# Linear attention as 24 groups of two pairs of heads, its matmuls on four 64x64 quarters, ahead of a gated MLP

## The chip, the cores and the metric

The kernel runs on one core of one Trainium2 chip. The core has a matrix engine (PE, with its weight loads shown as PEld), three engines for elementwise work (DVE, ACT, POOL), a queue for transfers (SP), a working memory of 128 partitions, and eight banks of 512 float32 columns per partition in which matmul results land (PSUM). The metric is device microseconds of one execution, the median of several runs.

## The reference, cut to what matters

There are 4 batches, 8 heads, 768 tokens and 48 channels per head. Attention keeps a 48x48 state for each batch and head; each token reads the state and its own contribution, weighted by the bonus `u`, and then decays the state by `w`:

```
for t in range(S):
    kt, vt, rt = (k[:, :, t], v[:, :, t], r[:, :, t])
    cur = np.einsum('bhd,bhe->bhde', u[None] * kt, vt)
    y[:, :, t] = np.einsum('bhd,bhde->bhe', rt, state + cur)
    state = w[None, :, :, None] * state + np.einsum('bhd,bhe->bhde', kt, vt)
```

Its output, 3072 tokens of 384 channels, goes through a gated MLP (called MoE in the code) with 1536 hidden channels:

```
gate = 1.0 / (1.0 + np.exp(-(x @ w_gate)))
val = x @ w_val
return (gate * val @ w_out).astype(np.float32)
```

## The kernel before, in words

**Attention.** The tokens are cut into 12 chunks of 64. A *burst* is one chunk of one pair of heads, all four batches: 48 bursts, four per chunk, in the order of the list `bursts`. With keys multiplied by inverse powers of the decay and queries by powers (table `tabk`), the attention inside a chunk becomes one masked score matrix of 64x64 for each batch and head, and everything earlier sits in the state. For burst n:

- `decayed` (L206) multiplies the keys by the table on DVE (L209), writes the decayed queries into the tile T on POOL (L212, a few on DVE) and multiplies query by key for the bonus on POOL (L215). `decayed_by_token` (L219) decays the keys in their token layout on POOL (L222).
- `bonus` (L224) multiplies by `u` and sums over channels on DVE (L228, L229). `diag` (L231) writes the sums as a diagonal matrix into the other half of T, in eight ACT instructions (L234).
- `scores` (L239) forms k times q for eight batch-and-head pairs: one head uses array rows 0 to 47 and output partitions 64 to 127, the other rows 64 to 111 and output partitions 0 to 63 (L245, L246). `outer` (L249) forms k times v for the state in the same two opposite corners (L255, L256).
- `post` (L258) copies the scores where the mask allows, over the diagonal, into T on DVE (L262), and decays and adds to the state, which lies in the tile vz beside the values, on DVE (L271, L273).
- `apply` (L278) multiplies state and values, stacked in the rows, by decayed queries and scores, stacked in the same way: eight matmuls over up to 128 rows, with two column halves (L283, L284). `to_x` (L286) splits the result into a rounded part (ACT, L300) and a rest (DVE, L301). For the fourth pair of heads these go to a separate tile xs, from which transfers on SP fill gaps in x (`fill`, L305).

**MLP.** Six tiles of 512 tokens (two chunks each) times 12 slices f of 128 hidden channels. An *item* is one slice of one tile. `up` (L323) is 18 matmuls in the float32r type (weights split into a high and a low part, three products for each of three row blocks, for gate and value). `gate` (L338) is a sigmoid on ACT (L343), a product on DVE (L344), a rounded copy on ACT (L345) and a rest on POOL (L346). `down` (L348) is nine matmuls into three accumulator banks (L356). The first tile runs its first four slices in halves of 256 tokens, eight half-width items and eight full ones. `store` (L365) copies the accumulators out in two halves (L368 on ACT, L369 on DVE) and sends them (L370).

**Weights** arrive as float64 words, are scaled on ACT (L175), joined to float32 in three DVE instructions (L181 to L183), rounded on ACT (L190) and subtracted on POOL (L191), in two halves for each of 12 slices. All of this falls into the first part of the run. `LOADW` and `DECW` say at which step each slice is loaded and decoded.

**Order.** The order on PE and SP is written out by hand; the other engines' order is chosen by the scheduler. `plan` lists the steps: five bursts alone (`PRE`), then items, with a burst in each of the first 11 and later in those which `SPREAD` marks (eight of twelve). In a step, `up` comes first (from the tenth step on), then the burst's scores and outer products, `apply` of the burst before, and `down` of the item before. Matmul results other than the accumulators share a ring of five single banks: `up` takes two, scores two, `apply` one.

Loads of a burst are one transfer of r and k in both layouts (L74), and for each chunk two transfers of v (L77, L78).

Of the kernel before, what the change touches and what calls it, by code (L numbers as in the profile page):

```python
# [10 lines left out]
F32 = mybir.dt.float32  # L11
# [9 lines left out]
P = 128  # L21
C = 64
# [8 lines left out]
PRE, HALF = NP + 1, 4  # L31
SPREAD = [1, 1, 1, 0, 1, 1, 1, 0, 1, 1, 0, 0]
EARLY = 9
LOADW = (-1, 1, 3, 4, 7, 9, 10, 11, 12, 13, 14, 15)
DECW = (1, 4, 5, 6, 9, 10, 11, 12, 13, 14, 15, 16)

U_POOL, R_DVE = range(3), range(4)
TILES = [[c, c + 1] for c in range(0, NC, 2)]
# [3 lines left out]
def rwkv_then_moe(ctx: ExitStack, tc: tile.TileContext, wd, un, rk, vn, wt, out):  # L42
# [6 lines left out]
    op = ctx.enter_context(tc.tile_pool(name="op", bufs=3))  # L49
    ps = ctx.enter_context(tc.tile_pool(name="ps", bufs=5, space=PSUM))  # L50
# [3 lines left out]
    att = main.enter_context(tc.tile_pool(name="att", bufs=4))  # L54
    att3 = main.enter_context(tc.tile_pool(name="att3", bufs=4))
    xp = main.enter_context(tc.tile_pool(name="xp", bufs=2))
    xsp = main.enter_context(tc.tile_pool(name="xsp", bufs=1))
# [6 lines left out]
    wu = const.tile([P, 2, NP], F32, name="wu")  # L64
    nc.sync.dma_start(out=wu, in_=wd)
    w = wu[:, 0]


    inp = {}
    vz = [const.tile([P, NP, 2, B, 64], F32, name=f"vz{i}") for i in range(2)]  # L70

    def load(c, p):
        inp[c, p] = att.tile([P, 2 * CT + 2 * B * D], F32, name="inp")
        nc.sync.dma_start(out=inp[c, p], in_=rk[c, p])  # L74

    def load_v(c):
        nc.sync.dma_start(out=vz[c % 2][64:128, :, 0], in_=vn[c, 64:128])  # L77
        nc.sync.dma_start(out=vz[c % 2][0:64, :, 1], in_=vn[c, 0:64])  # L78

    uns = const.tile([P, NP, D], F32, name="uns")  # L80
    ORDER = [NP - 1] + list(range(NP - 1))
    bursts = [(c, p) for c in range(NC) for p in ORDER]
    load(*bursts[0])
    load_v(0)
    nc.sync.dma_start(out=uns, in_=un)
    load(*bursts[1])
# [9 lines left out]
    cmask = causal.bitcast(I32)  # L96

    nc.vector.memset(vz[1][64:128, :, 1], 0.0)
    for t in (vz[0][0:64, :, 0], vz[0][64:128, :, 1], vz[1][0:64, :, 0]):
        nc.gpsimd.memset(t, 0.0)  # L100
    table = const.tile([P, 1], F32, name="table")
# [4 lines left out]
    pw = const.tile([P, NP, 97], F32, name="pw")  # L106
# [3 lines left out]
    def power(lo, n, by):  # L110
        nc.vector.tensor_tensor(
            pw[:, :, lo + 1 : lo + 1 + n], pw[:, :, 1 : 1 + n],
            pw[:, :, by : by + 1].broadcast_to([P, NP, n]), ALU.mult,
        )
# [7 lines left out]
    tabk = const.tile([P, NP, C], F32, name="tabk")  # L122
    nc.vector.tensor_copy(tabk[:, :, 0:32], pw[:, :, 31::-1])

    def inverses(p):
        nc.vector.reciprocal(tabk[:, p, 32:64], pw[:, p, 1:33])

    tabn = const.tile([P, NP, D], F32, name="tabn")
    flag = const.tile([1, 1], I32, name="flag")

    def token_table():

        power(32, 32, 32)
        power(64, 32, 64)
        tnat_in = hp.tile([P, 512], F32, name="sg").rearrange("q (p a j) -> q p a j", p=NP, a=2)
        for p in range(NP):
            nc.vector.tensor_copy(
                tnat_in[:, p], pw[:, p, 95:31:-1].unsqueeze(1).broadcast_to([P, 2, C])
            )
        tps = ps.tile([P, NP, P], F32, name="ring")  # L140
        for p in range(NP):
            nc.tensor.transpose(
                out=tps[:, p], in_=tnat_in[:, p].rearrange("q a j -> q (a j)"), identity=ident
            )
        nc.scalar.copy(out=tabn[0:64], in_=tps[0:64, :, 64:112])
        nc.scalar.copy(out=tabn[64:128], in_=tps[64:128, :, 0:48])

    def range_flag():
        good = const.tile([P, NP], F32, name="good")
# [4 lines left out]
        count = ps.tile([P, 512], F32, name="ring")  # L154
        nc.tensor.matmul(count[0:1, 0:NP], ones, good, start=True, stop=True)
        nc.vector.tensor_reduce(total, count[0:1, 0:NP], axis=mybir.AxisListType.X, op=ALU.add)
        nc.vector.tensor_scalar(flag, total, float(P * NP), None, ALU.is_lt)
# [34 lines left out]


    xt, xs, T, q, sc, yp = {}, {}, {}, {}, {}, {}

    def bc_b(ap):
        n, k = ap.shape
        return ap.unsqueeze(1).broadcast_to([n, B, k])

    def parts(n):  # L200
        c, p = bursts[n]
        t = inp[c, p][:, 0 : 2 * CT].rearrange("q (a b i) -> q a b i", a=2, b=B)
        u = inp[c, p][:, 2 * CT :].rearrange("q (a b d) -> q a b d", a=2, b=B)
        return c, p, t, u, vz[c % 2][:, p]

    def decayed(n):  # L206
        c, p, t, u, z = parts(n)
        T[n] = att3.tile([P, 2, B, C], F32, name="T")
        nc.vector.tensor_tensor(t[:, 1], t[:, 1], bc_b(tabk[:, p]), ALU.mult)  # L209
        for lo, k in ((0, 0), (64, 1)):  # L210
            eng = nc.vector if k and n in R_DVE else nc.gpsimd
            eng.tensor_tensor(  # L212
                T[n][lo : lo + 64, k], t[lo : lo + 64, 0], bc_b(tabk[lo : lo + 64, p, ::-1]), ALU.mult
            )
        nc.gpsimd.tensor_tensor(u[:, 0], u[:, 0], u[:, 1], ALU.mult)  # L215
        if n in U_POOL:
            nc.gpsimd.tensor_tensor(u[:, 0], u[:, 0], bc_b(uns[:, p]), ALU.mult)

    def decayed_by_token(n):  # L219
        c, p, t, u, z = parts(n)  # L220
        if c < NC - 1:
            nc.gpsimd.tensor_tensor(u[:, 1], u[:, 1], bc_b(tabn[:, p]), ALU.mult)  # L222

    def bonus(n):  # L224
        c, p, t, u, z = parts(n)
        q[n] = att.tile([P, B], F32, name="q")
        if n not in U_POOL:
            nc.vector.tensor_tensor(u[:, 0], u[:, 0], bc_b(uns[:, p]), ALU.mult)  # L228
        nc.vector.tensor_reduce(q[n], u[:, 0], axis=mybir.AxisListType.X, op=ALU.add)  # L229

    def diag(n):  # L231
        for lo, k in ((64, 0), (0, 1)):
            for b in range(B):
                nc.scalar.activation(  # L234
                    T[n][lo : lo + 64, k, b], ident[lo : lo + 64, lo : lo + 64], AF.Copy,
                    scale=q[n][lo : lo + 64, b : b + 1],
                )

    def scores(n):  # L239
        c, p, t, u, z = parts(n)  # L240
        s1 = ps.tile([P, 512], F32, name="ring")
        s2 = ps.tile([P, 512], F32, name="ring")
        for b in range(B):
            cs = slice(b * C, (b + 1) * C)
            nc.tensor.matmul(s1[64:128, cs], t[0:48, 1, b], T[n][0:48, 0, b], start=True, stop=True)  # L245
            nc.tensor.matmul(s2[0:64, cs], t[64:112, 1, b], T[n][64:112, 1, b], start=True, stop=True)  # L246
        sc[n] = s1, s2

    def outer(n):  # L249
        c, p, t, u, z = parts(n)  # L250
        s1, s2 = sc[n]
        if c < NC - 1:
            for b in range(B):
                cs = slice(256 + b * D, 256 + (b + 1) * D)
                nc.tensor.matmul(s1[64:112, cs], u[0:64, 1, b], z[0:64, 1, b, 0:D], start=True, stop=True)  # L255
                nc.tensor.matmul(s2[0:48, cs], u[64:128, 1, b], z[64:128, 0, b, 0:D], start=True, stop=True)  # L256

    def post(n):  # L258
        c, p, t, u, z = parts(n)
        s1, s2 = sc.pop(n)  # L260
        for lo, k, s in ((64, 0, s1), (0, 1, s2)):
            nc.vector.copy_predicated(  # L262
                T[n][lo : lo + 64, k], bc_b(cmask[lo : lo + 64, lo : lo + 64]),
                s[lo : lo + 64, 0:256].rearrange("q (b i) -> q b i", b=B),
            )
        if c < NC - 1:
            zn = vz[(c + 1) % 2][:, p]
            for lo, k, s in ((0, 0, s2), (64, 1, s1)):
                kv = s[lo : lo + 48, 256:448].rearrange("q (b e) -> q b e", b=B)
                if c == 0:  # L270
                    nc.vector.tensor_copy(zn[lo : lo + 48, k, :, 0:D], kv)  # L271
                    continue
                nc.vector.scalar_tensor_tensor(  # L273
                    zn[lo : lo + 48, k, :, 0:D], z[lo : lo + 48, k, :, 0:D], pw[lo : lo + 48, p, 64:65],
                    kv, ALU.mult, ALU.add,
                )

    def apply(n):  # L278
        c, p, t, u, z = parts(n)
# [6 lines left out]
    def to_x(n):  # L286
# [25 lines left out]
        elif ti and p < 3 and c == TILES[ti][-1]:  # L312
            fill(p, slice(0, CT * len(TILES[ti])))

# [315 lines left out]
```

## Time and profile before

| | |
|---|---|
| median of 3 runs | 611.71 us (611.42 to 612.87) |
| the profiled execution | 615.25 us |
| its span, first to last instruction | 613.4 us |
| mean granted clock of PE | 0.977 |
| busy in the span: PE, DVE, ACT, POOL | 562.6, 282.8, 242.3, 292.3 us |
| PE matmul records | 4298, of which 2052 MLP |
| moved by transfers | 50.42 MB |

Rows of the profile that group instructions give line, engine and operation, output and inputs with their shapes, a count, then busy time in us and the mean of one in ns, then the engine's idle time ahead of them and what ended it. Timeline rows give the start and the length in us, engine, line, operation and, in brackets, the idle time before. Rows of stretches give, for each engine, busy time and the number of instructions. Shapes are partitions x columns. A float32 matmul stands in the trace as two records, a float32r one as one.

### The profile page before, as it was taken

The numbers are of one execution on the slowest core, as the hardware profiler recorded it, in microseconds if no ns is written. First come the engines' busy times: TensorE is split into PE (matmuls) and PEld (weight loads), VectorE is DVE, ScalarE is ACT, GpSimd is POOL, SyncE is SP. The second block draws the span as 40 slices with busy tenths as digits, with TensorE's granted clock in tenths as the row PEclk, the third lists the DMA queues.
The fourth block names the chain that finished last, engine by engine and source line by source line (L and its number), as shares of the span: only waits on it lengthen the run. The fifth ranks groups of instructions, "written<-read, shape, count | busy, mean of one in ns | idle before, by whom it ended". The sixth has DMA issues, their size and how long they took to land. (4 is left out here: it accounts for less than half of the span.)

```text
span 613.4 us, 10938 instructions
## 1 busy us (share of the span) xinstructions
PE 562.6 (92%) x4298; PEld 454.1 (74%) x4298; DVE 282.8 (46%) x568; ACT 242.3 (39%) x656; POOL 292.3 (48%) x298
## 2 busy tenths in 40 slices
PE   1667788889899999999999999999999999999995
PEld 1556787667777777777777777877777777888883
DVE  8889998998235334145334145334243322111011
ACT  2737776545324343335334136334145322211111
POOL 7587999886426345237335138335333311212121
PEclk9997898979899999999999999999999999999998
DMA  7393666333021122331122331211331100100001
GB/s 237 116 320 103 231 239 219 134 116 81 0 85 60 32 65 69 82 109 35 46 56 67 80 113 32 76 57 42 73 113 30 31 10 10 37 24 1 0 1 56
DMA packets 21369, 50.42 MB, mean 82 GB/s; under 512 B 2656, under 2 KB 9312, under 8 KB 21312
## 3 DMA queue, kind: packets, MB, share of 16 engines
q1 hardware_dynamic: 21312, 49.66, 27.0%
q8 instruction: 36, 0.59, 0.4%
q14 instruction: 21, 0.17, 0.1%
HBM read 42.57 MB, written 4.72 MB: 77 GB/s over the span
## 5 line engine op out<-in xcount | busy, mean ns | idle before, releaser
L331 PE MATMUL ring<-xt,whi 128*128 128x512 f32 (+1 forms) x912 | 280.2, 390 | 0.0
L331 PEld LDWEIGHTS ring<-xt,whi 128*128 128x128 f32 x912 | 173.9, 195 | 36.7
L346 POOL TENSOR_TENSOR h<-sg,h 128x512 fp32r<-128x512 f32 (+1 forms) x76 | 97.6, 1285 | 198.9 <-ACT h L345 198.5
L331 PE MATMUL ring<-xt,wlo 128*128 128x512 f32 (+1 forms) x456 | 179.4, 393 | 6.9 <-POOL wlo L191 4.0
L344 DVE TENSOR_TENSOR sg<-ring,sg 128x512 f32<-128x512 f32 (+1 forms) x76 | 50.2, 660 | 211.8 <-PE ring L331 203.4
L234 ACT ACTIVATE T<-ident,q 64x64 f32<-64x64 f32 x384 | 102.2, 335 | 64.4 <-DVE q L229 63.0
L356 PE MATMUL acc<-h,whi 128*128 128x512 f32 (+1 forms) x456 | 115.5, 383 | 7.4 <-POOL h L346 7.0
L331 PEld LDWEIGHTS ring<-xt,wlo 128*128 128x128 f32 x456 | 89.2, 196 | 26.2 <-POOL wlo L191 4.4
L212 POOL TENSOR_TENSOR T<-inp,tabk 64x256 f32<-64x256 f32 x92 | 82.0, 891 | 49.3 <-DMA inp<-in_rk 31.7
L356 PEld LDWEIGHTS acc<-h,whi 128*128 128x128 f32 x456 | 83.4, 189 | 25.9 <-POOL h L346 8.1
L343 ACT ACTIVATE sg<-ring 128x512 f32<-128x512 f32 (+1 forms) x76 | 43.4, 572 | 125.5 <-PE ring L331 125.5
L345 ACT CAST h<-sg 128x512 fp32r<-128x512 f32 (+1 forms) x76 | 45.3, 596 | 110.1 <-DVE sg L344 110.0
L356 PE MATMUL acc<-h,wlo 128*128 128x512 f32 (+1 forms) x228 | 70.4, 408 | 0.1
L215 POOL TENSOR_TENSOR inp<-inp 128x192 f32<-128x192 f32 x48 | 34.4, 717 | 49.6 <-DMA inp<-in_rk 47.9
L209 DVE TENSOR_TENSOR inp<-inp,tabk 128x256 f32<-128x256 f32 x48 | 28.5, 593 | 61.8 <-DMA inp<-in_rk 61.8
L191 POOL TENSOR_TENSOR wlo<-wf,whi 128x576 fp32r<-128x576 f32 x24 | 42.8, 1793 | 10.3 <-ACT T L234 4.8
L262 DVE COPY_PREDICATED T<-causal,ring 64x256 f32<-64x256 int32 x96 | 43.0, 448 | 4.9 <-PE ring L256 2.4
L356 PEld LDWEIGHTS acc<-h,wlo 128*128 128x128 f32 x228 | 38.6, 190 | 8.9 <-ACT h L345 0.5
L245 PEld LDWEIGHTS ring<-T,inp 48*64 48x64 f32 x384 | 28.9, 145 | 17.2 <-issue 14.4
L283 PE MATMUL ring<-T,vz 128*64 128x64 f32 x384 | 36.3, 242 | 3.7 <-DVE T L262 2.1
L245 PE MATMUL ring<-T,inp 48*64 48x64 f32 x384 | 36.7, 238 | 2.3 <-issue 2.0
L246 PE MATMUL ring<-T,inp 48*64 48x64 f32 x384 | 35.3, 237 | 3.5 <-DVE vz L273 2.1
(54 smaller groups left out, 497.2 us busy)
## 6 DMA issues: line engine op xcount, KB each, us to landing
inp<-in_rk SPq DMA_DIRECT2D x48, 448.0 KB, 3.9
wr<-in_wt SPq DMA_DIRECT2D x24, 576.0 KB, 6.4
vz<-in_vn SPq DMA_DIRECT2D x24, 256.0 KB, 4.5
out_y<-o SPq DMA_DIRECT2D x18, 256.0 KB, 2.4
xt<-xs SPq DMA_DIRECT2D x30, 64.0 KB, 2.3
xt<-xs SPq DMA_DIRECT2D x12, 32.0 KB, 2.1
uns<-in_un SPq DMA_DIRECT2D x1, 96.0 KB, 5.2
wu<-in_wd SPq DMA_DIRECT2D x1, 4.0 KB, 1.6
```

The costliest lines, as they stand in the source:

```text
L191: nc.gpsimd.tensor_tensor(wlo[f][:, c], g, whi[f][:, c], ALU.subtract)
L212: eng.tensor_tensor(T[n][lo : lo + 64, k], t[lo : lo + 64, 0], bc_b(tabk[lo : lo + 64, p, ::-1]), ALU.mult)
L234: nc.scalar.activation(T[n][lo : lo + 64, k, b], ident[lo : lo + 64, lo : lo + 64], AF.Copy, scale=q[n][lo : lo + 64, b : b + 1],)
L245: nc.tensor.matmul(s1[64:128, cs], t[0:48, 1, b], T[n][0:48, 0, b], start=True, stop=True)
L262: nc.vector.copy_predicated(T[n][lo : lo + 64, k], bc_b(cmask[lo : lo + 64, lo : lo + 64]), s[lo : lo + 64, 0:256].rearrange("q (b i) -> q ...
L283: nc.tensor.matmul(y[0:64, cs], z[:, 0, b], T[n][:, 0, b], start=True, stop=True)
L331: nc.tensor.matmul(o[:, self.cols], w[a][:, g * DM + kt * P : g * DM + (kt + 1) * P], self.x[:, kt, b, self.cols], start=(k == 0), stop=(k ...
L343: nc.scalar.activation(sg[:, c], a[:, c], AF.Sigmoid)
L344: nc.vector.tensor_tensor(sg[:, c], b[:, c], sg[:, c], ALU.mult)
L345: nc.scalar.copy(out=h[:, 0, c], in_=sg[:, c])
L346: nc.gpsimd.tensor_tensor(h[:, 1, c], sg[:, c], h[:, 0, c], ALU.subtract)
L356: nc.tensor.matmul(self.acc[d][:, self.cols], w[a][:, 2 * DM + d * P : 2 * DM + (d + 1) * P], h[:, b, self.cols], start=(f == 0 and k == 0 ...
```

## The change

Attention is regrouped. A *group* is one chunk of two pairs of heads, all four batches: 24 groups, two per chunk, sixteen batch-and-head pairs each. Two batches lie in rows 0 to 63 and two in rows 64 to 127 (index be); output goes to two column halves (gm). Every attention matmul now uses one 64x64 quarter of the array.

- The inputs come as two transfers per group: r and k by channel (512 KB) and k and v by token (400 KB), rearranged on the host.
- `prepare` makes decayed queries on POOL (512 columns), keys times u on ACT (four instructions of 128 columns) and decayed keys on DVE (512 columns); `prepare_tokens` the decayed token keys on POOL (384 columns).
- `scores` makes two sets of 64x64 products, decayed keys with decayed queries, and keys times u with plain queries, whose diagonal is the bonus: 32 matmul calls per group. `keep` copies both sets through two masks into a score tile, in two DVE instructions of 512 columns. The products, sums and diagonals of the bonus fall away.
- The state has its own tile. `apply` has 16 calls by state, 16 for the outer products and 16 by scores; a drain of PE stands after those by state. `advance` updates the state in four DVE instructions of 96 columns (one copy in the first chunk).
- `to_x` splits 512 columns at once, straight into a wider x; the tile xs is gone.
- The ring becomes two tiles of two banks each: one pair for an `up`, one for a group's scores, one for its `apply`.
- MLP items begin after two groups. The other groups go into fixed slots: six in the first tile's items, then four in each tile (items 0, 3, 6, 9). In a slot item PE runs `up`, the scores, `down` of the item before, and `apply`.
- Weights are loaded two items and decoded one item ahead, one slice per item from the start.
- Output tiles have two buffers instead of three.

The path for decays out of range, which does not run with these inputs, is adapted and left out below, as are the host's rearrangements.

```diff
+SLOTS0 = {0: 2, 2: 3, 4: 4, 7: 5, 10: 6, 13: 7}
+SLOTS = (0, 3, 6, 9)
+LOADW = (-2, -1, 0, 1, 2, 3, 4, 5, 6, 7, 8, 9)
+DECW = (-1, 0, 1, 2, 3, 4, 5, 6, 7, 8, 9, 10)
...
-    op = ctx.enter_context(tc.tile_pool(name="op", bufs=3))
-    ps = ctx.enter_context(tc.tile_pool(name="ps", bufs=5, space=PSUM))
+    op = ctx.enter_context(tc.tile_pool(name="op", bufs=2))
+    ps = ctx.enter_context(tc.tile_pool(name="ps", bufs=2, space=PSUM))
...
+    def two_banks():
+        return ps.tile([P, 2, 512], F32, name="ring")
...
+    def prepare(n):
+        c, g = GROUPS[n]
+        t = dec[n] = adk.tile([P, 2, 512], F32, name="dec")
+        r, k = chan[n][:, 0], chan[n][:, 1]
+        tab = tabk[:, 4 * g : 4 * g + 4]
+        nc.gpsimd.tensor_tensor(v4(t[:, 0]), v4(r), bc2(tab[:, :, ::-1]), ALU.mult)
+        for m in range(4):
+            cs = slice(128 * m, 128 * m + 128)
+            nc.scalar.activation(
+                t[:, 1, cs], k[:, cs], AF.Copy, scale=wu[:, 1, 4 * g + m : 4 * g + m + 1]
             )
+        nc.vector.tensor_tensor(v4(k), v4(k), bc2(tab), ALU.mult)
+
+    def prepare_tokens(n):
+        c, g = GROUPS[n]
         if c < NC - 1:
+            k = toks[n][:, 0, 0 : 8 * D]
+            nc.gpsimd.tensor_tensor(v4(k), v4(k), bc2(tabn[:, 4 * g : 4 * g + 4]), ALU.mult)
+
+    def scores(n):
+        sc = ga[n] = two_banks()
+        t, r, k = dec[n], chan[n][:, 0], chan[n][:, 1]
+        for kk, rr, at in ((k, t[:, 0], 0), (t[:, 1], r, 256)):
+            for p, p2 in PP:
+                o = at + (2 * p + p2) * C
+                for be, gm in QUARTERS:
+                    row, cs = slice(64 * be, 64 * be + D), (4 * p + 2 * (be ^ gm) + p2) * C
+                    nc.tensor.matmul(
+                        sc[64 * gm : 64 * gm + 64, be, o : o + C],
+                        kk[row, cs : cs + C], rr[row, cs : cs + C], start=True, stop=True,
+                    )
+
+    def keep(n):
+        sc, t = ga.pop(n), score[n % 2]
+        for m, at in ((0, 0), (1, 256)):
+            nc.vector.copy_predicated(
+                t.rearrange("q (b m i) -> q b m i", b=2, m=4),
+                masks[:, m].bitcast(I32).unsqueeze(1).unsqueeze(1).broadcast_to([P, 2, 4, C]),
+                sc[:, :, at : at + 256].rearrange("q b (m i) -> q b m i", m=4),
+            )
+
+    def apply(n):
...
+        units = []
+        if c:
+            units += [(by_state, p, p2) for p, p2 in PP]
+        if c < NC - 1:
+            units += [(outer, p, p2) for p, p2 in PP]
+        units += [(by_scores, p, p2) for p, p2 in PP]
+        turned = False
+        for f, p, p2 in units:
+            if f is not by_state and c and not turned:
+
+                nc.tensor.drain()
+                turned = True
+            for half in range(2):
+                f(half, p, p2)
+
+    def advance(n):
...
+        for p in range(2):
+            for s in range(2):
+                at = (2 * p + s) * n2
+                nc.vector.scalar_tensor_tensor(
+                    st[:, at : at + n2], st[:, at : at + n2],
+                    pw[0:112, 4 * g + 2 * p + s, 64:65],
+                    y[0:112, s, 256 + p * n2 : 256 + (p + 1) * n2], ALU.mult, ALU.add,
                 )
...
+    for i, it in enumerate(items):
+        m = moe_of(it)
+        m.up(it[2])
+        n = slot.get(i)
         if n is not None:
             scores(n)
...
+        m.gate(it[2])
+        if n is not None:
+            keep(n)
+        if pend:
+            finish(pend)
+        pend = it
+        if n is not None:
+            apply(n)
+            to_x(n)
+            advance(n)
+            ready(n + 1)
+        weights(i)
```

More of the change, by code (lines that the diff above doesn't have):

```diff
@@ L153, in range_flag @@
         nc.vector.tensor_tensor(good, w, pw[:, :, 1], ALU.is_equal)
[L154 to L157, printed above, removed]
+        count = two_banks()[:, 0]
+        nc.tensor.matmul(count[0:1, 0:N2], ones, good, start=True, stop=True)
+        nc.vector.tensor_reduce(total, count[0:1, 0:N2], axis=mybir.AxisListType.X, op=ALU.add)
+        nc.vector.tensor_scalar(flag, total, float(P * N2), None, ALU.is_lt)
     W3, WH = 3 * DM, 3 * DM // 2
@@ L239, in scores @@
[L239 to L276, printed above, removed]
@@ L278, in apply, with decode @@
-    def apply(n):
-        c, p, t, u, z = parts(n)
-        y = yp[n] = ps.tile([P, 512], F32, name="ring")
-        for b in range(B):
-            cs = slice(b * C, (b + 1) * C)
-            nc.tensor.matmul(y[0:64, cs], z[:, 0, b], T[n][:, 0, b], start=True, stop=True)
-            nc.tensor.matmul(y[64:112, cs], z[0:112, 1, b, 0:D], T[n][0:112, 1, b], start=True, stop=True)
+    def decode(f):
+        for j in range(2):
+            scale_words(f, j)
+        for j in range(2):
+            join_words(f, j)
+        split_weights(f)
@@ L426, in finish, with weights @@
             store(accs[ti], slice(TILES[ti][0], TILES[ti][-1] + 1))
-    for i, (n, it) in enumerate(plan):
-        later = [k for k, _ in plan[i + 1 :] if k is not None]
-        while later and nload < min(len(bursts), later[0] + 3):
-            load(*bursts[nload])
-            nload += 1
+    def weights(i):
         for f in [f for f, at in enumerate(LOADW) if at == i]:
             load_weights(f)
-        nn = n + 2 if n is not None and n + 2 < len(bursts) else None
-        m = it and moe_of(it)
-        early = i < EARLY
-        if it and not early:
-            m.up(it[2])
-        if nn is not None:
-            decayed(nn)
-            decayed_by_token(nn)
-        if it and not early:
-            m.gate(it[2])
+        for f in [f for f, at in enumerate(DECW) if at == i]:
+            decode(f)
@@ new lines, in rwkv_then_moe, with ready @@
+    inverses(1)
+    load(1)
+    weights(-2)
+    prepare(0)
+    token_table()
+    prepare_tokens(0)
+    scores(0)
+    inverses(0)
+    load(2)
+    weights(-1)
+    prepare(1)
+    prepare_tokens(1)
+    keep(0)
+    apply(0)
+    scores(1)
+    advance(0)
+    to_x(0)
+    keep(1)
+    apply(1)
+    to_x(1)
+    advance(1)
+    nload, nprep = 3, 2
+    def ready(n):
+        nonlocal nload, nprep
+        while nload < min(len(GROUPS), n + 2):
+            load(nload)
+            nload += 1
+        while nprep < min(len(GROUPS), n + 1):
+            prepare(nprep)
+            prepare_tokens(nprep)
+            nprep += 1
@@ L459, in rwkv_then_moe @@
-        if nn is not None:
-            bonus(nn)
-        for fj in [(f, j) for f, at in enumerate(DECW) if at == i for j in range(2)]:
-            scale_words(*fj)
-        if nn is not None:
-            diag(nn)
-        for fj in [(f, j) for f, at in enumerate(DECW) if at == i for j in range(2)]:
-            join_words(*fj)
-            if fj[1] == 1:
-                split_weights(fj[0])
-        if it and early:
-            m.up(it[2])
-            m.gate(it[2])
-        if pend_m:
-            finish(pend_m)
```

328 lines of the change are left out of this document (167 added, 161 removed).

## The prediction

> **What bounds the kernel now.** I read the stretches first, cut at the places where the kind of work changes: engine busy time, then granted clock.
>
> ```profile
> 0.00:42.00 42.00, 17.92 (x244) 14.91 (x244) 34.60 (x77) 19.88 (x58) 27.80 (x39) 1.00 0.68 218
> 42.00:152.50 110.50, 93.60 (x894) 79.71 (x894) 102.94 (x171) 68.77 (x189) 96.34 (x84) 0.91 0.52 167
> 152.50:170.00 17.50, 14.97 (x58) 12.10 (x59) 3.74 (x6) 6.23 (x15) 8.84 (x9) 0.90 0.00 0
> 170.00:606.00 436.00, 435.64 (x3103) 347.30 (x3102) 140.66 (x314) 146.80 (x393) 159.33 (x169) 1.00 0.18 50
> ```
>
> The columns are the stretch, PE, PEld, DVE, ACT, POOL, clock, DMA share, GB/s. Two stages have two different limits. Up to 152.5 us DVE is the fullest engine: 102.94 of 110.5 us. From 170 us to 606 us PE never rests: 435.64 of 436. So the start is worth what DVE is spared, and the rest what the PE stream is shortened. The timeline of PE gives the two marks and the length of one plain MoE item.
>
> ```profile
> 44.06 0.58 PE L331 MATMUL ring<-xt,wlo 128*128 128x256 f32 x1
> ...
> 169.88 0.40 PE L331 MATMUL ring<-xt,wlo 128*128 128x512 f32 x1
> ...
> 528.70 0.40 PE L331 MATMUL ring<-xt,wlo 128*128 128x512 f32 x1
> ...
> 534.95 0.40 PE L331 MATMUL ring<-xt,wlo 128*128 128x512 f32 x1
> ```
>
> MoE starts at 44.06, the second tile at 169.88 (stage A ends, stage B begins), the last tile at 528.70, its second item at 534.95. A plain item is 6.25 us. Between 169.88 and 528.70 lie 48 items: 358.82 - 48 x 6.25 = 58.8 us are attention, 32 bursts of 1.84 us.
>
> Now one burst, in the timeline of PE:
>
> ```profile
> 301.93 0.63 PE L331 MATMUL ring<-xt,whi 128*128 128x512 f32 x2
> 302.50 0.27 PE L245 MATMUL ring<-T,inp 48*64 48x64 f32 x1
> 302.50 0.27 PE L246 MATMUL ring<-T,inp 48*64 48x64 f32 x1
> 302.60 0.22 PE L245 MATMUL ring<-T,inp 48*64 48x64 f32 x1
> 302.66 0.22 PE L245 MATMUL ring<-T,inp 48*64 48x64 f32 x1
> ...
> 303.01 0.20 PE L255 MATMUL ring<-vz,inp 64*48 64x48 f32 x1
> ...
> 303.32 0.20 PE L255 MATMUL ring<-vz,inp 64*48 64x48 f32 x1
> ...
> 303.47 0.27 PE L283 MATMUL ring<-T,vz 128*64 128x64 f32 x1
> ...
> 303.92 0.22 PE L283 MATMUL ring<-T,vz 128*64 128x64 f32 x1
> 304.07 0.50 PE L356 MATMUL acc<-h,wlo 128*128 128x512 f32 x1
> ```
>
> Every float32 call leaves two records. L245 and L246 use opposite corners of the array and start together; then a pair follows every 0.058 us (302.60 to 303.01 in seven steps). The 48-column outer products step by 0.045 (303.01 to 303.32 in seven). The apply pair, L283 with L284, uses all rows on both column halves and steps by 0.064 (303.47 to 303.92 in seven, the first one long). So a step lasts as long as its moving columns, whatever shares it. Eight steps of each are 0.47 + 0.36 + 0.51 = 1.34 us; from the end of the MoE matmuls (302.39: the second of the two of 301.93 starts 0.23 later, and the next could 0.23 after that) to 304.07 are 1.68, so three changes of array shape cost 0.11 us each.
>
> **Stage B, on PE.** A group stands for two bursts. It has 32 score calls (bonus included), 16 by state, 16 outer, 16 by scores. Two records each, four quarters at a time: 16, 8, 8 and 8 steps, that is 32 x 0.058 + 8 x 0.045 = 2.2 us if all four quarters run together. Two visits make four changes, 0.45. The added drain is in no row: 0 at best, at worst a matmul's own 0.22 (302.60) plus a change of 0.11, 0.33; I take 0.25, nearer the worst, since the pipe must empty. With what the mean burst has over the one above (1.84 - 1.68 = 0.16) a group is 3.1 us. Sixteen groups: 49.6 against 58.8, **9 us less**.
>
> Whether four quarters run together no row shows. For it: opposite corners do, and the apply pair already streams two different moving operands through all 128 rows, the traffic of four quarters. Here the Trainium skill speaks against the change: its page TensorE: Matmul & The Clock Gate, in Part 3 (Packing small matmuls), says that a weight load overlaps a matmul in flight only where the row group differs. By it two quarters on the same rows would take turns. The trace has it otherwise:
>
> ```profile
> 303.47 0.17 PEld L284 LDWEIGHTS ring<-T,vz 112*48 112x48 f32 x2
> 303.52 0.14 PEld L283 LDWEIGHTS ring<-T,vz 128*64 128x64 f32 x1
> ```
>
> The load for L283 at 303.52 runs beside its own matmul of 303.47, on the same 128 rows.
>
> **Stage A, on DVE.** The groups of DVE up to 152.5 us, with busy time and mean, and from later the 512-column product:
>
> ```profile
> L183 DVE SCALAR_TENSOR_TENSOR wf<-wr,wf 128x576 int32<-128x576 int32 x24 | 25.4, 1057 | 0.3
> L182 DVE SCALAR_TENSOR_TENSOR wf<-wr,wf 128x576 int32<-128x576 int32 x24 | 23.6, 981 | 0.2
> L181 DVE TENSOR_SCALAR wf<-wf 128x576 int32<-128x576 int32 x24 | 19.6, 817 | 4.0 <-ACT wf L175 3.9
> L262 DVE COPY_PREDICATED T<-causal,ring 64x256 f32<-64x256 int32 x32 | 14.2, 444 | 0.9
> L209 DVE TENSOR_TENSOR inp<-inp,tabk 128x256 f32<-128x256 f32 x20 | 14.2, 710 | 3.3 <-DMA inp<-in_rk 3.3
> L228 DVE TENSOR_TENSOR inp<-inp,uns 128x192 f32<-128x192 f32 x16 | 9.9, 619 | 3.6 <-POOL inp L215 3.6
> L273 DVE SCALAR_TENSOR_TENSOR vz<-vz,pw,ring 48x192 f32<-48x192 f32 x24 | 9.7, 406 | 0.0
> L229 DVE TENSOR_REDUCE q<-inp 128x4 f32<-128x192 f32 x19 | 6.4, 343 | 0.8 <-POOL inp L217 0.7
> L301 DVE TENSOR_TENSOR xt<-ring,xt 112x256 fp32r<-112x256 f32 (+1 forms) x14 | 5.8, 412 | 0.1
> L212 DVE TENSOR_TENSOR T<-inp,tabk 64x256 f32<-64x256 f32 x4 | 4.9, 1222 | 0.1
> L271 DVE COPY vz<-ring 48x192 f32<-48x192 f32 x8 | 2.8, 350 | 0.0
> ```
>
> ```profile
> L344 DVE TENSOR_TENSOR sg<-ring,sg 128x512 f32<-128x512 f32 x36 | 24.9, 691 | 116.4 <-PE ring L331 110.8 <-ACT sg L343 5.6
> ```
>
> The first three are the weights, 68.6 us, untouched. The other eight are attention: 67.9 us. From L301 (0.412 at 256 columns) to L344 (0.691 at 512) a column costs 1.09 ns. The eight groups of this stage then need: decayed keys, between L209's 0.71 and twice that, say 1.1 x 8 = 8.8; masked copies, 0.444 + 0.28 = 0.72 x 16 = 11.5; split of y, 0.69 x 10 = 6.9 (two groups do it in two parts); state, 0.406 less 96 columns = 0.30 x 4 x 6 = 7.2, and twice 0.55 for the first chunk; 2 more for tables twice as wide. Sum 37.5, so DVE is spared **30 us**: its decoding would end at 122 instead of 152.5, and stage A at 139 with the same 17.4 us after it.
>
> What must not wait inside a slot item of stage B: the ring is now two pairs of banks. Apply takes the pair that up just filled, so it waits for the gate, whose sigmoid and product take 0.57 (L343) and 0.69 (L344):
>
> ```profile
> L343 ACT ACTIVATE sg<-ring 128x512 f32<-128x512 f32 (+1 forms) x76 | 43.4, 572 | 125.5 <-PE ring L331 125.5
> ```
>
> It comes after the scores (1.2 us) and nine down matmuls (a third of 6.25, 2.1 us): 3.3 us of cover for about 1.4. The masked copies, twice 0.72 behind that product, end near 3 us, before by-scores at 4.5; the split of y and the four state updates, 0.7 + 1.2, hide behind the next up (4.2 us). Without this cover the price would be 1 to 2 us a group.
>
> PE sets a floor. MoE can begin after two groups instead of six bursts; first weights are there early already:
>
> ```profile
> 29.27 3.28 POOL L191 TENSOR_TENSOR wlo<-wf,whi 128x576 fp32r<-128x576 f32 x2 [4.76 <-ACT T L234]
> ```
>
> They end at 32.55, behind POOL's attention work, so I put the first up at 28. Eight half-width items (27 matmuls at about 0.118, half a plain item's 0.23) are 25.5, eight full ones 50, six groups 18.6: 94, at the granted 0.91 of the clock 103, ending at 131. POOL and ACT get lighter too:
>
> ```profile
> L234 ACT ACTIVATE T<-ident,q 64x64 f32<-64x64 f32 x384 | 102.2, 335 | 64.4 <-DVE q L229 63.0
> L212 POOL TENSOR_TENSOR T<-inp,tabk 64x256 f32<-64x256 f32 x92 | 82.0, 891 | 49.3 <-DMA inp<-in_rk 31.7
> ```
>
> Four scaled copies a group replace sixteen L234, and two POOL products of 512 and 384 columns replace eight, four of them L212. On SP, a weight load now stands behind the fills of x, which wait for a group's split of y: a few us in the first items, where DVE would wait for words. Between 139 by DVE and these added waits (that queue, and up waiting for gate or masked copy behind a decoding step of about 1 us, with two pairs instead of five banks) I take 145: **25 us less**, from 0 to 39.
>
> **The tail** pays. Output tiles have two buffers instead of three, and the third output waits for the first store.
>
> ```profile
> 606.03 2.15 SPq L370 DMA_DIRECT2D out_y<-o  x3
> ...
> 606.55 0.37 ACT L368 COPY o<-acc 128x256 f32<-128x256 f32 x1 [0.31 <-PE acc L356]
> ```
>
> ```profile
> out_y<-o SPq DMA_DIRECT2D x18, 256.0 KB, 2.4
> ```
>
> 606.03 + 2.4 = 608.4 against 606.55: **2 us more** (0 to 2.5).
>
> **Sum.** Profiled execution 615.25 (span 613.4 and 1.85 around it): 615.25 - 9 - 25 + 2 = 583. It stands 3.5 above the median of 611.71, so the median becomes 580.
>
> **Rivals.** *Quarters take turns.* If only two quarters run at a time, 40 steps become 80: a group costs 2 x 2.2 + 0.9 = 5.3, stage B 85 instead of 58.8, 26 more; stage A, with eight such groups on PE, shortens by only 15. 611.7 + 26 - 15 + 2 = 625. It decides from a step of about 0.09 us, where 24 groups of 38 longer steps eat up the 32. For it: no row shows four at once, and the densest rows, the outer products, issue four records (two loads, two matmuls) in 0.045 us, at which rate the eight of a full step take 0.09. Against it: the apply pair, and the weight load at 303.52. The rule of the Trainium skill given above would bring this case about. *The start does not shorten.* Ring and SP queue give back all that DVE gains: 611.7 - 9 + 2 = 605. For it: PE is 93.6 of 110.5 busy already; against: DVE's 102.94. *The start reaches PE's floor* of 131: 611.7 - 9 - 39 + 2 = 566.
>
> **How the numbers follow.** Forecast 0.66, turns 0.14, unshortened start 0.14, floor 0.06. About 0.3%, 1.8 us, is what a measurement can tell from no change. All but the turns are faster; a sliver lies within: 0.84, 0.02, 0.14. The range runs from 562 (floor, less drain) to 607, leaving out the turns.
>
> **What would show it.** Right: score records in fours within 0.03 us, stepping 0.058; slot items 3.1 us over 6.25; first up near 28, second tile near 145; DVE's attention up to then near 37; the third output copy 2 us late. Wrong: fours spread over 0.1 us or more; gaps before apply or up naming gate, masked copy or state; a second tile near 170.

## The result and the profile after

The changed kernel takes 626.21 us (626.12 to 627.75, 4 runs) against 612.29 us (611.42 to 613.19, 4 runs) before: 1.0233 times as long, 95% interval 1.021 to 1.0257. The forecast was 580. The time lies on the forecast of one rival, 625 for quarters that take turns, but the trace shows that this mechanism did not happen.

The stretches of the changed kernel, with the columns as in the prediction (stretch, PE, PEld, DVE, ACT, POOL, clock, DMA share, GB/s):

```profile
0.00:40.30 40.30, 8.88 (x261) 7.94 (x261) 26.43 (x41) 13.94 (x30) 20.13 (x27) 1.00 0.42 157
40.30:125.00 84.70, 51.45 (x863) 47.00 (x864) 68.40 (x90) 37.30 (x73) 47.85 (x32) 0.82 0.50 187
125.00:183.40 58.40, 53.92 (x521) 42.94 (x520) 20.52 (x38) 15.72 (x30) 21.02 (x15) 0.97 0.14 40
183.40:538.10 354.70, 351.78 (x3795) 281.43 (x3794) 93.80 (x180) 89.01 (x181) 95.66 (x74) 1.00 0.16 52
538.10:624.10 86.00, 77.73 (x334) 62.16 (x332) 10.76 (x18) 17.00 (x31) 16.84 (x13) 0.98 0.05 19
```

They are cut at PE's timeline, at the first `up`, the first of the second tile and the first of the last tile:

```profile
40.29 0.55 PE L386 MATMUL ring<-xt,wlo 128*128 128x256 f32 x1 [10.36 <-ACT xt L353]
...
66.91 0.58 PE L386 MATMUL ring<-xt,wlo 128*128 128x256 f32 x1 [15.72 <-POOL wlo L199]
...
183.43 0.40 PE L386 MATMUL ring<-xt,wlo 128*128 128x512 f32 x1
...
538.10 0.40 PE L386 MATMUL ring<-xt,wlo 128*128 128x512 f32 x1
```

So stage A grew from 169.88 to 183.43 (13.5 us more), stage B shrank from 358.82 to 354.67 (4.2 less), and the last tile with the tail grew from 84.7 to 86.0 (1.3 more). Together that is 10.7, the difference of the spans (613.4 and 624.1); the medians differ by 13.9, since the profiled execution before was 3 us slower than its median. But for the 1.3 of the tail the loss is all in the start. There PE waits 10.36 us ahead of the first `up` and 15.72 ahead of the third, and in the 84.7 us from the first `up` to 125 it is at work in 51.45.

One group inside stage B, in PE's timeline:

```profile
299.38 0.69 PE L247 MATMUL ring<-dec,chan 48*64 48x64 f32 x32
299.90 0.65 PE L247 MATMUL ring<-chan,dec 48*64 48x64 f32 x32
300.48 0.96 PE L409 MATMUL acc<-h,wlo 128*128 128x512 f32 x3
...
302.73 0.68 PE L270 MATMUL ring<-dec,state 48*64 48x64 f32 x32
303.56 0.61 PE L270 MATMUL ring<-toks 64*64 64x48 f32 x30
```

32 records of one set of scores last 0.69 us with the last one's own 0.22: eight steps of 0.058, four quarters to a step. By turns there would be sixteen, over 1.1 us. The drain shows between the last rows: the last record by state starts at 302.73 + 0.68 - 0.22 = 303.19, the first outer product 0.37 later, where a step is 0.058. This gap holds the change from 48 to 64 rows as well.

What held the start, in the waits up to 125 us (waiting engine and line, what it waited for, total us, times, longest), and in SP's own up to 130:

```profile
PE ring L386 <- POOL wlo L199: 15.7, 1, 15.7
PE ring L270 <- DVE score L255: 14.4, 5, 6.6
```

```profile
SPq L358 <- DVE score L255: 20.8, 1, 20.8
...
SPq L358 <- DVE xt L354: 15.7, 1, 15.7
```

SP's timeline shows what stood behind those waits (L178 is half a weight slice, L358 a fill of x, L81 a group's r and k):

```profile
5.07 1.16 SPq L178 DMA_DIRECT2D wr<-in_wt  x2
27.35 4.93 SPq L358 DMA_DIRECT2D xt<-xt  x6
32.40 0.51 SPq L81 DMA_DIRECT2D chan<-in_ch  x1
...
49.21 4.72 SPq L358 DMA_DIRECT2D xt<-xt  x6
54.03 0.53 SPq L81 DMA_DIRECT2D chan<-in_ch  x1
...
55.08 1.85 SPq L178 DMA_DIRECT2D wr<-in_wt  x4
```

From 6.2 to 55.1 us not one weight slice is sent for. The third slice's loads, which only need free memory, stand behind the fills of two groups, and those wait for the groups' split of y. (The first row of waits names a masked copy; but what the fills read, and what ended just then on DVE, at 27.32, is the split, L354.)

### The profile page after: what moved, and what is told of

Its sections match the earlier page's. It is cut to its first block, busy times and chain, and to the rows that moved or that the text cites. A ratio compares the mean times of both kernels' runs of the same rounds, so it can differ in the third digit from the quotient of the medians.

```text
span 624.1 us, 13029 instructions
## 1 busy us (share of the span) xinstructions
PE 543.8 (87%) x5770; PEld 441.5 (71%) x5770; DVE 219.9 (35%) x365; ACT 173.0 (28%) x343; POOL 201.5 (32%) x161
## 5 line engine op out<-in xcount | busy, mean ns | idle before, releaser
L386 PE MATMUL ring<-xt,wlo 128*128 128x512 f32 (+1 forms) x456 | 180.5, 396 | 34.9 <-POOL wlo L199 15.7
L409 PE MATMUL acc<-h,wlo 128*128 128x512 f32 (+1 forms) x228 | 67.3, 395 | 2.5 <-ACT h L398 2.5
L225 POOL TENSOR_TENSOR dec<-chan,tabk 128x512 f32<-128x512 f32 x24 | 32.7, 1364 | 80.9 <-DMA chan<-in_ch 76.6
L409 PEld LDWEIGHTS acc<-h,wlo 128*128 128x128 f32 x228 | 40.9, 190 | 12.3 <-ACT h L398 3.4
L228 ACT ACTIVATE dec<-chan,wu 128x128 f32<-128x128 f32 x96 | 31.1, 392 | 65.3 <-DMA chan<-in_ch 57.4
L231 DVE TENSOR_TENSOR chan<-chan,tabk 128x512 f32<-128x512 f32 x24 | 19.8, 824 | 73.6 <-ACT dec L228 73.6
L255 DVE COPY_PREDICATED score<-masks,ring 128x512 f32<-128x512 int32 x48 | 35.8, 745 | 1.0 <-PE ring L247 0.3
L270 PE MATMUL ring<-score,toks 64*64 64x64 f32 (+1 forms) x768 | 18.6, 233 | 15.2 <-DVE score L255 14.4
L237 POOL TENSOR_TENSOR toks<-toks,tabn 128x384 f32<-128x384 f32 x22 | 29.2, 1332 | 6.9 <-DMA toks<-in_tk 3.8
L354 DVE TENSOR_TENSOR xt<-ring,xt 112x512 fp32r<-112x512 f32 (+1 forms) x26 | 17.9, 688 | 32.5 <-ACT xt L353 32.2
L270 PEld LDWEIGHTS ring<-score,toks 64*64 64x64 f32 (+1 forms) x768 | 15.4, 136 | 16.2 <-DVE score L255 15.4
L353 ACT CAST xt<-ring 112x512 fp32r<-112x512 f32 (+1 forms) x26 | 15.2, 586 | 39.5 <-PE ring L270 34.1
```

What stands on the lines that cost most here:

```text
L225: nc.gpsimd.tensor_tensor(v4(t[:, 0]), v4(r), bc2(tab[:, :, ::-1]), ALU.mult)
L228: nc.scalar.activation(t[:, 1, cs], k[:, cs], AF.Copy, scale=wu[:, 1, 4 * g + m : 4 * g + m + 1])
L237: nc.gpsimd.tensor_tensor(v4(k), v4(k), bc2(tabn[:, 4 * g : 4 * g + 4]), ALU.mult)
L255: nc.vector.copy_predicated(t.rearrange("q (b m i) -> q b m i", b=2, m=4), masks[:, m].bitcast(I32).unsqueeze(1).unsqueeze(1).broadcast_to ...
L270: nc.tensor.matmul(y[64 * half : 64 * half + m, bank, cs], lhsT, rhs, start=first, stop=stop, skip_group_check=True,)
L386: nc.tensor.matmul(o[:, g, self.cols], w[a][:, g * DM + kt * P : g * DM + (kt + 1) * P], self.x[:, kt, b, self.cols], start=(k == 0), stop ...
```

## The experiments

Theory A: SP's queue, in which the weight loads stand behind the fills, starves the decoding. The other theories look at the order of the work on DVE, ACT and POOL: the changed kernel decodes earlier and has fewer buffers for the matmul results, so that a decoding step ahead of a masked copy or a gate now holds PE (where an expectation gives a further letter, it says there what it stands for). The plainest rival to all of them is that the engines' sums set the time, whatever stands ahead of what. All ratios are to the kernel before, run in turn on the same chip; "second tile" is its first `up`, 183.43 in the changed kernel and 169.88 before.

**Loads early.**

```diff
-LOADW = (-2, -1, 0, 1, 2, 3, 4, 5, 6, 7, 8, 9)
+LOADW = (-2, -1, -1, -1, -1, -1, 0, 0, 1, 1, 2, 2)
```

> The load of the weight slices 1 to 5 is issued before the first fills of x instead of behind them; nothing else differs from the changed kernel. Theory A (the SP queue starves the start): in the changed kernel no weight is issued between 6.2 and 55.1 us, and the third up waits from 50.9 to 66.9 us for it. With the words there early, that wait of 16 us goes, decoding fills the idle DVE between 27 and 60 us, and the second tile begins near 167 us instead of 183.4: about 610 us. The first up stays near 40. Theory B (the order on DVE and ACT is what holds the start: scores kept late, an ACT instruction in front of the split of y): the loads change little, under 5 us, since the first up stays at 40 and the work behind it is bound by DVE from there on: about 622 us.

613.91 us, ratio 1.0008 (0.9989 to 1.0027). The second tile begins 11.2 us earlier, and the 15.7 us wait for the third slice is gone:

```profile
172.21 0.40 PE L386 MATMUL ring<-xt,wlo 128*128 128x512 f32 x1
```

The queue is shown as the cause of that wait. That it alone is worth the 11.2 us is not shown: with the other list the scheduler also chose another order (103 of DVE's 365 instructions stand in another place than in the changed kernel), and the first `up` came no earlier (41.55). 167 was not reached, and the gain forecast for the start is still missing.

**Program order.** DVE, ACT and POOL, too, run in the order in which the program is written (the names of the engines are shortened here).

```diff
-tc.manual_schedule(engines={PE, SP})
+tc.manual_schedule(engines={PE, SP, DVE, Activation, Pool})
```

> DVE, ACT and POOL take their instructions in the order in which the program writes them, instead of the scheduler's order; loads as in the changed kernel. Theory B: the decoding of slice 1 no longer stands before the second masked copy on DVE, and the key products of the fourth group no longer before the split of y on ACT (8.8 us of waiting for a load), so the first up comes at about 31 us instead of 40.3. Theory A: the third up still waits for slice 2, which is issued behind the fills of the third group; these come 9 us earlier too, so 9 us at most are won and the wait of about 16 us stays: about 617 us. If neither holds: no change, 626 us.

620.69 us, 1.0119 (1.0077 to 1.0161). Now the first `up` starts where the prediction had it, near 28, and another wait has come, below it in this kernel's waits:

```profile
28.51 0.58 PE L386 MATMUL ring<-xt,wlo 128*128 128x256 f32 x1 [2.04 <-ACT xt L353]
```

```profile
PE ring L386 <- POOL wlo L199: 24.8, 3, 9.8
```

The 12 us ahead of the first `up` (40.29 to 28.51) were thus the scheduler's order. In the changed kernel's ACT timeline it is seen directly: the keys of a later group, waiting for their load, stand ahead of the split of y that the first items need.

```profile
36.14 1.28 ACT L228 ACTIVATE dec<-chan,wu 128x128 f32<-128x128 f32 x4 [8.79 <-DMA chan<-in_ch]
37.32 0.56 ACT L353 CAST xt<-ring 48x512 fp32r<-48x512 f32 x1
```

**Both.** The last edit and the early loads.

> Early loads of slices 1 to 5 and program order on DVE, ACT and POOL together. If both theories hold and add up: first up near 31 us, no wait of the third up, second tile near 158 us, 626 - 9 - 16 = 601 us, which is faster than the kernel before. If only A holds: as with early loads alone, about 610. If DVE is the limit anyway (95 us of work before the second tile, full from about 12 us on): the second tile cannot begin before about 150 us, 593 us at best.

621.43 us, 1.0126 (1.0083 to 1.0169). They don't add up: with the order fixed, the early loads gained nothing (620.69 us without them). The wait for split weights is 24.3 us, as without the early loads: in program order a slice is decoded one item ahead and handed from ACT to DVE to ACT to POOL, so that it comes too late however early it is loaded.

**Loads ahead of the fills in the items, too,** and the same with the first two groups alone in program order:

> As with early loads, and the weight slices 6 to 11 are issued at the start of items 0, 1 and 2 instead of at their ends, so that SP sends them ahead of the fills and of the group's next loads. With early loads alone DVE was busy only 11 of the 20 us from 60 to 80 us, with 291 GB/s moving, and full again from 80 to 120. If the late words caused that dip, it goes, and the second tile begins near 164 instead of 172.2: about 606 us. If the dip has another cause (PE's own work between the items, or the scheduler's order), no more than 2 us change: 612 to 614 us.

> As with the loads first, and DVE, ACT and POOL take the instructions of the two groups ahead of the first item in program order, then the scheduler's order again. Program order throughout brought the first up to 28.5 us against 41.6, but lost it by decoding one slice at a time, each handed from engine to engine. If the order of the first two groups alone is what costs 13 us, the first up comes near 29 and the second tile 8 to 13 us earlier than with the loads first: about 596 us. If the sum of DVE's work is the limit behind it (95 to 119 us of it before 180), the first up is early but the second tile moves by less than 4 us.

616.39 us, 1.0055 (1.0038 to 1.0072), and 622.17 us, 1.0145 (1.0125 to 1.0164): both missed. Already in the first experiment PE no longer waits for split weights, which fits that more loads ahead of the fills gained nothing; and an order fixed for a part of the start alone was worse.

**Quarter by quarter.** The score matmuls are issued four in a row for each quarter instead of one for each in turn; all else as in the changed kernel.

```diff
-            for p, p2 in PP:
-                for be, gm in QUARTERS:
+            for be, gm in QUARTERS:
+                for p, p2 in PP:
```

> The changed kernel with the score matmuls written out quarter by quarter: eight calls... four calls of one quarter in a row, then four of the next, instead of one call for each of the four quarters in turn. The same 32 calls per group. If quarters run together whatever the order (PE reaching ahead over other quarters' instructions), nothing changes: 626 us, score steps of four at 0.058 us. If matmuls start in program order and only neighbours in different quarters overlap, most of the 64 records of a group follow each other singly at 0.058: up to 3.7 instead of 0.93 us for the scores, 24 x 2.6 = 60 us at most: up to 690 us. That is the price of the rival in which quarters take turns, made on purpose.

655.95 us in a single run, span 654.0 against 624.1. A group in its PE timeline:

```profile
312.56 1.36 PE L247 MATMUL ring<-dec,chan 48*64 48x64 f32 x29
313.71 0.27 PE L247 MATMUL ring<-chan,dec 48*64 48x64 f32 x1
313.76 0.22 PE L247 MATMUL ring<-dec,chan 48*64 48x64 f32 x1
313.82 0.22 PE L247 MATMUL ring<-chan,dec 48*64 48x64 f32 x1
313.82 0.22 PE L247 MATMUL ring<-dec,chan 48*64 48x64 f32 x1
313.88 0.22 PE L247 MATMUL ring<-chan,dec 48*64 48x64 f32 x1
...
315.18 0.96 PE L409 MATMUL acc<-h,wlo 128*128 128x512 f32 x3
```

From the first score to the `down` behind them 2.62 us instead of 1.10 (299.38 to 300.48): four quarters of one set take 1.15 (312.56 to 313.71), 0.29 each. A run of eight records alone would take eight steps, 0.46. Where one quarter's run ends and the next one's begins, between 313.76 and 313.88, both step by 0.06 side by side; the rest of the time one quarter steps alone. So quarters overlapped only where their calls are neighbours, two at a time. Beside it, the changed kernel's step shows that its four quarters really ran together.

**Decoding emitted later,** with the early loads and without:

```diff
+DECW = (-1, 0, 1, 2, 6, 7, 8, 9, 10, 11, 12, 13)
```

> Early loads, and the slices 4 to 11 are decoded three items later (at items 6 to 13 instead of 3 to 10; slice 4 is first used at item 8). Theory C: it is the order of the work on DVE, ACT and POOL that holds the start, not its sum and not the loads: decoding for full items stands before the attention work and gates of the half-width items 0 to 7, so that the first full item begins at 114.6 with early loads, and behind it PE alone needs 58 us. With later decoding the first full item comes near 95 and the second tile near 153: about 595 us. Rival D: what DVE has to do in all is the limit wherever it is put; then slices 8 to 11 come too late, up waits for them in items 12 to 15, and the second tile stays within 4 us of 172: 610 to 618.

> The same later decoding with the loads of the changed kernel. Theory C with the loads a second, separate cause: items 0 to 3 still lose the 16 us until slice 2 is there (second tile 183.4 in the changed kernel), but items 4 to 7 come faster (31 us in the changed kernel, 20 by PE's own work): 10 us less, about 616. If the loads are all that matters, no change: 626.

613.64 us, 1.0001 (0.9982 to 1.0019), and 625.93 us, 1.0192 (1.016 to 1.0224). Neither says anything for or against the order of decoding. With the early loads the scheduler put the instructions of DVE, ACT and POOL in the same order as without the edit; without them a few changed places (6 of 365 on DVE, 14 of 343 on ACT, 3 of 161 on POOL). So under the scheduler this edit of `DECW` moved the decoding hardly at all.

**In order and further ahead.** Both edits of the third run, with slice 1 decoded before the first item, slices 2 and 3 one item earlier and 4 to 11 two later.

```diff
+DECW = (-1, -9, 0, 1, 5, 6, 7, 8, 9, 10, 11, 12)
...
 advance(1)
+decode(1)
```

> Early loads, program order on DVE, ACT and POOL, each of the slices 1 to 3 decoded one item further ahead than in the changed kernel, slices 4 to 11 two items later. In program order the first up came at 28.5, but up then waited 25 us for slices 1 to 3, which were begun one item ahead and handed from engine to engine in 8 to 10 us. Theory C: with the decoding one item further ahead that wait goes: first up near 29, first full item near 85, second tile near 145: about 587 us, faster than the kernel before. Rival D: second tile near 172 or later, 612 or more.

605.94 us, 0.987 (0.9842 to 0.9898): faster than both kernels, though not the 587 expected. The second tile begins at 165.97. With the same sums and the same loads as the third run, the order alone is worth 15.5 us. The longest waits left on PE up to 172 us, apart from one in the set-up (9.3):

```profile
PE ring L270 <- DVE sg L397: 12.9, 4, 4.6
...
PE ring L270 <- DVE score L255: 7.6, 1, 7.6
```

**Three tries at the 12.9 us.** `apply` takes the banks that `up` filled and waits for the gate's product, ahead of which a decoding step stands on DVE. The first moves whole slices to other items (`DECW = (-1, -9, 0, 1, 4, 5, 5, 7, 8, 8, 10, 11)`), the second issues the rounded copy and the subtraction of a slice behind the next gate, the third the six joins as well:

```diff
         m.gate(it[2])
         if n is not None:
             keep(n)
+        while unjoined:
+            join(unjoined.pop())
```

> The kernel of the run before (all engines in program order, weight slices loaded early, decoded further ahead: 605.94 us) with the decoding steps moved so that in items 4 to 15 none stands in DVE's order ahead of a slot item's gate: slices 4 to 11 are decoded behind items 4, 5, 5, 7, 8, 8, 10, 11 instead of 5 to 12. Theory C (what is lost in the start is the order of work on DVE, not its sum): the 12.9 us in which PE waits in four slot items for the gate's product ahead of apply fall to about 3; the second tile begins near 156 instead of 166.0, and the time is about 596 us. Rival (the sum of DVE's work now sets the end, whatever stands ahead of what): the wait only moves to other items, the second tile stays within 3 us of 166 and the time within 603 to 609.

> The kernel of 605.94 us (all engines in program order, loads early, decoding further ahead) with one edit: for slices 4 to 11 the rounded copy on ACT and the subtraction on POOL are issued behind the next item's gate instead of ahead of it, so that ACT's sigmoid no longer stands behind a copy that waits for DVE's three joins. If the wait of apply for the gate's product (12.9 us in four slot items) is ACT's queue, handed from engine to engine, it falls below 5 us, the second tile begins near 158 instead of 166.0 and the time is about 598 us. Rival (the joins on DVE themselves, 4.2 us a slice ahead of the product, make the wait): it stays above 9 us and the time within 603 to 609.

> The kernel of 605.94 us with one edit: for slices 4 to 11 the six joining instructions on DVE (4.2 us), the rounded copies on ACT and the subtractions on POOL are issued behind the next item's gate and masked copies instead of ahead of the gate; the scaling on ACT stays where it was. If the joins in DVE's order make apply wait for the gate's product (12.9 us in four slot items), that wait goes to below 3 us, the second tile begins near 156 instead of 166.0, and the time is 594 to 600 us. Rival (whatever stands ahead of what, the engines need this long, and the wait moves, as in the two runs before): PE waits as long elsewhere, for split weights or the split of y, and the time stays within 603 to 610.

The first gave 609.78 us, 0.9923 (0.9905 to 0.9941); as its rival said, the wait moved (its 609 us was just passed): two slices in a row now hold the scores of the next slot item, which wait 14.2 us for the gate before. The second gave 608.2 us, 0.9926 (0.9898 to 0.9954), with a wait of 17.5 us: ACT's queue was not it. Its timeline shows why. The sigmoid is done at 85.84 + 0.36 (ACT), and the product comes only behind the joins (DVE):

```profile
85.84 0.36 ACT L401 ACTIVATE sg<-ring 128x256 f32<-128x256 f32 x1
```

```profile
89.36 0.76 DVE L191 SCALAR_TENSOR_TENSOR wf<-wr,wf 128x576 int32<-128x576 int32 x1
90.03 0.42 DVE L402 TENSOR_TENSOR sg<-ring,sg 128x256 f32<-128x256 f32 x1
```

The third gave 600.53 us (600.28 to 602.6), 0.9786 (0.9764 to 0.9807), the fastest of all. Its stretches, the last one cut at its own second tile:

```profile
40.30:125.00 84.70, 70.34 (x1030) 61.67 (x1024) 53.54 (x90) 36.35 (x75) 37.80 (x32) 0.86 0.34 132
125.00:161.20 36.20, 31.94 (x277) 25.40 (x276) 22.93 (x35) 15.18 (x28) 19.97 (x15) 0.95 0.22 64
```

Between 40 and 125 us PE is now at work 70.34 us instead of 51.45, and DVE 53.54 instead of 68.40. The second tile begins at 161.24, 22.2 us ahead of the changed kernel. The expected 156 was missed: the wait for the gate fell from 12.9 to 8.0 us only.

```profile
PE ring L278 <- DVE sg L405: 8.0, 3, 2.8
```

## Why the prediction was wrong

**What held.** The forecast step of 0.058 us with four quarters at once, and with it the fall of the rival by turns. DVE's terms: masked copy 0.735 us (0.72 forecast), split of y 0.69 (0.69), state 0.31 (0.30), decayed keys 0.93 (1.1), and their sum, nearly. DVE is busy 115.4 us up to 183.4 (26.43 + 68.40 + 20.52) where before it was 141.3 up to 170 (34.60 + 102.94 + 3.74): 26 us spared, where 30 were forecast. The third output copy came late: the last tile and tail grew by 1.3 us, with 2 forecast.

**Sized wrong, in stage B.** PE's timeline has the first `up` of a slot item, of the item behind it and of the one after that:

```profile
295.10 0.40 PE L386 MATMUL ring<-xt,wlo 128*128 128x512 f32 x1
...
304.64 0.50 PE L386 MATMUL ring<-xt,wlo 128*128 128x512 f32 x1
...
310.99 0.40 PE L386 MATMUL ring<-xt,wlo 128*128 128x512 f32 x1
```

A slot item lasts 9.54 us and the one behind it 6.36 (the usual lengths in this stage), against 6.25 twice: a group is 3.40 us, not 3.1. The 2.2 us of steps stand; the drain's gap is 0.37, about 0.31 more than a step, where 0.25 was put down, and the rest lies in first steps and changes of shape, which no run tells apart. So stage B gave 4.2 us of the 9.

**The step that failed.** "DVE is spared 30 us: its decoding would end at 122 instead of 152.5, and stage A at 139 with the same 17.4 us after it." The changed kernel's last join on DVE, and what PE was at by then, in the two timelines:

```profile
131.97 0.76 DVE L191 SCALAR_TENSOR_TENSOR wf<-wr,wf 128x576 int32<-128x576 int32 x1
```

```profile
128.46 0.47 PE L386 MATMUL ring<-xt,wlo 128*128 128x512 f32 x1 [1.72 <-DVE state L329]
...
138.86 0.63 PE L386 MATMUL ring<-xt,wlo 128*128 128x512 f32 x1
```

The first half of the step came out 10.7 us late: decoding ends at 132.7. The second half does not follow, and costs three times as much. From there to the second tile lie 50.7 us instead of 17.4, and most of them are PE's own work: `up` of the tenth of sixteen items, begun at 128.46, was just ending. The `down` behind it, that of the ninth item, with a wait ahead of it, lasted to 138.86 (6.2), and then came six items of 6.25 and two groups of 3.40 (44.3). Before, PE kept up with the decoding and had 17.4 us left at its end. The forecast moved one engine's end and carried the other's lag along, unproved. The rival nearest to this is the unshortened start, 605 us: ring and queue gave back more than DVE gained. That the time lies beside the 625 of the turns is chance.

PE's lag can be added up against the floor of 131 that the prediction gave. Its first `up` came 12.3 us later than the 28 assumed. From then on its waits in the timeline, 15.72 ahead of the third `up` the largest, sum to 36.8 us. 131 + 12.3 + 36.8 = 180.1, of the 183.4 measured. The 3.3 us left are of the size of two terms that no run separates: groups of 3.40 us instead of 3.1 (six of them, 2 us), and PE's granted clock, 0.88 on the mean of the two stretches (0.82 and 0.97) instead of 0.91, by which the floor's 94 us of work take some 3 us more (both estimates). The floor was nearly sound; what was missing was a reason why PE should come near it.

**The queue** was seen and mis-sized: "a weight load now stands behind the fills of x, which wait for a group's split of y: a few us in the first items". The loads stood there from 6.2 to 55.1 us, and the wait at the end of it was 15.7. Moving the loads ahead, with the order that the scheduler then chose, gave back 11.2 us of the 13.5 that stage A had lost; in program order it gave back nothing. The fills can't go before the split of y, so the price should have been read from when that split comes, not from how long a fill takes.

**The order on DVE, ACT and POOL** was not in the prediction beyond "a decoding step of about 1 us" ahead of a gate. A slice is six joins, 4.2 us. With two pairs of banks, whatever waits behind them holds PE: masked copies in the scheduler's order, gates in program order. The runs show it by its price: the same instructions in another order, with the loads early, gave 621.43, 605.94 and 600.53 us.

Not settled: how near to 131 the start can come. In the last run PE still waits on gates (8.0), masked copies (7.6), split weights (7.5) and smaller things, and no run took those away. Nor was a third output tile tried, nor a third pair of banks, for which the three accumulators and two pairs leave one bank of eight.

## What to carry to other kernels

Sparing the fullest engine moves the end of a stage only by as much as the next engine can follow: work out what that engine has left at the new end, item by item, rather than keep the old lag. On a queue that is served in order, price an edit by the release time of what it is put behind. And where buffers are cut, lay out anew which work stands ahead of the small instruction that frees them: here 4.2 us of decoding, moved behind a product of 0.4 to 0.7 us, gave 5.4 us (605.94 to 600.53).

## What the runs showed of the hardware

A 64x64 quarter alone steps its 64-column float32 records by 0.058 us, and four neighbours on four quarters take the same step together, two of them on the same rows with their weight loads (32 records in eight steps). The order of the calls decides whether that happens (1.10 or 2.62 us for the same 64 records).

The six joins took very different times for the same work. Here are their groups in DVE's time up to the second tile, in the changed kernel and then in the run in program order:

```profile
L190 DVE SCALAR_TENSOR_TENSOR wf<-wr,wf 128x576 int32<-128x576 int32 x24 | 25.4, 1059 | 0.5
L191 DVE SCALAR_TENSOR_TENSOR wf<-wr,wf 128x576 int32<-128x576 int32 x24 | 24.2, 1009 | 0.3
L189 DVE TENSOR_SCALAR wf<-wf 128x576 int32<-128x576 int32 x24 | 21.3, 889 | 3.6 <-ACT wf L183 3.5
```

```profile
L190 DVE SCALAR_TENSOR_TENSOR wf<-wr,wf 128x576 int32<-128x576 int32 x24 | 19.0, 792 | 0.9
L191 DVE SCALAR_TENSOR_TENSOR wf<-wr,wf 128x576 int32<-128x576 int32 x24 | 18.2, 758 | 0.8
L189 DVE TENSOR_SCALAR wf<-wf 128x576 int32<-128x576 int32 x24 | 13.7, 570 | 8.6 <-ACT wf L183 8.6
```

70.9 us against 50.9, by order alone. In the changed kernel the third join took 0.75 us on the mean where no POOL instruction ran beside it (14 of 24) and 1.44 where one ran through at least 80% of it (9 of 24). An example, in the timelines of DVE and POOL:

```profile
14.87 1.43 DVE L191 SCALAR_TENSOR_TENSOR wf<-wr,wf 128x576 int32<-128x576 int32 x1
16.23 1.52 DVE L189 TENSOR_SCALAR wf<-wf 128x576 int32<-128x576 int32 x1
```

```profile
12.04 3.65 POOL L237 TENSOR_TENSOR toks<-toks,tabn 128x384 f32<-128x384 f32 x3 [3.07 <-ACT tabn L151]
15.66 1.77 POOL L225 TENSOR_TENSOR dec<-chan,tabk 128x512 f32<-128x512 f32 x1
```

The third join ends 0.61 us behind the first POOL row's end (16.30 and 15.69), the next slice half's first join 0.32 behind the second's (17.75 and 17.43). Alone, these two take 0.75 and 0.45, so that they end as if most of them came behind POOL's. The Trainium skill, page SBUF — State Buffer, section Who interferes with whom, says that a DVE instruction with two inputs in that memory contends with a GpSimd (POOL) instruction that reads it, for ports which one of them holds at a time. The trace agrees for the third join, which has two such inputs; the first has one, and no run shows why it waits too. The prediction counted the 68.6 us of joins as untouched; a plan that keeps POOL's work from beside them would spare DVE some 20 us, an estimate from the 70.9 and 50.9. The run in program order had these 20 us and still took 620.69 us.
